# Silu at a block's end moved by a section to ScalarE and GpSimd, and idle transposes at the start, in a fused attention and GEGLU kernel

## The chip, the cores and the metric

The kernel runs on one core of one Trainium2 chip. The core has five engines with their own instruction queues: TensorE (PE; its weight loads are listed as PEld), VectorE (DVE), ScalarE (ACT), GpSimd (POOL) and SyncE (SP), which issues nearly all DMA transfers. Each engine works through its queue in order and waits on semaphores for the others. The metric is the device time of one execution in microseconds (us); lower is better. Each kernel's time is the median of several executions.

## The reference

```python
x = A_x                                    # 1 x 2048 x 576
xn = _layernorm(x, axis=-1)
s = _A_ref(xn, A_wqkv, A_wo)               # attention, 32 heads of 18, output projection
g = _silu(_B_ref(xn, B_w_gate, B_w_up, B_w_down))
return x + s * g
...
def _B_ref(x, w_gate, w_up, w_down):       # hidden size 4608
    return (_gelu(x @ w_gate) * (x @ w_up)) @ w_down
```

`_gelu` is the tanh form. All data is float32.

## The kernel before

The 2048 tokens are worked in four blocks of 512 (`TB`, `NB`). Float32 products are made from pairs of rounded parts, a high and a low one (`hi`/`lo`, `wh`/`wl`, `hh`/`hl`, `dh`/`dl`), each split by two operations, on GpSimd in `split` (L91, L92) or on ScalarE and VectorE in `split_av` (L96, L97).

**First phase** (up to about 199 us). For each block, `load_x` fetches four tiles of 128 tokens, `norm` normalises them on VectorE (the last step is L196), ScalarE copies a strip of 64 columns (L198), and `transposes` turns them on TensorE: 20 transposes of 128x128 (L206) into five PSUM banks `pt`, in the order tile `j`, then bank `k`. So each bank is whole only after the fourth tile. `split_t` takes the banks to SBUF (L160, L161). Then `project` multiplies by the q and k weights (`mm_terms`, L152, bank `po`, three buffers) and `values_of` by the v weights. The identity `ident` of the transposes is made by GpSimd at the very start.

**Main phase.** TensorE's order is written by hand (`manual_schedule`); the other engines' queues are ordered by the scheduler, except where `keep_in_program_order` holds an instruction. The phase is a row of 144 *sections*, 36 for each block of the feed-forward part. A section `n` holds 27 pairs of gate and up matmuls (`gate_up`, L347), interleaved with attention's score matmuls (L632, then exp on ScalarE in L633) and row maximum matmuls (L605, then L606 on VectorE). After the pairs, `activate` computes gelu times up (L360 to L364); then TensorE does attention's value matmuls (L666) and the down matmuls (L377) of an earlier section. `down` is called twice for each pair of sections, for the token halves `js` = (0, 1) and (2, 3); VectorE copies (L381, first step of a block) or adds (L383) the result into the sums tile `Y` (128 x 4 x 576), in pieces of 128x288. `finish` splits the gelu product (`hh`, `hl`) and the down weights (`dh`, `dl`).

At the last step of blocks 0 to 2, `down` also makes the silu, by `gate`: tanh(y/2) on ScalarE (L354), then (tanh + 1) y on VectorE (L355), which is twice the silu; L505 takes the half later. The product goes in place into `Y`, and SyncE stores each 128x576 row block to the DRAM tile `ys` (L392). This happens at the end of two successive sections for each block: sections 36 and 37, 72 and 73, 108 and 109. The last block's sums are gated apart, at the end of the kernel (`finals`).

Later, eight pieces of 128x288 for each block, `load_xy` fetches `x` and `ys` into `xx` and `yy` (pool `op`; one and two buffers), and `project_o` computes the output projection and combines (L505 on VectorE, L506 on GpSimd).

SyncE's queue carries, in order, the key loads `KS`, query loads `q`, value loads `VS`, the raw weights (`raw`, two buffers shared by gate/up and down weights), and the stores.

Of the kernel before, what the change touches and what calls it, by code (L numbers as in the profile page):

```python
# [8 lines left out]
F32 = mybir.dt.float32  # L9
F32R = mybir.dt.float32r  # L10
AF = mybir.ActivationFunctionType
ALU = mybir.AluOpType
# [4 lines left out]
S, D, H, DH, F = 2048, 576, 32, 18, 4608  # L17
P = 128
NT = S // P
TB = 512  # L20
# [31 lines left out]
def f(ap):  # L52
    return ap.bitcast(F32)
# [13 lines left out]
def kernel(ctx: ExitStack, tc: tile.TileContext, x, wqkv, wo, w_gate, w_up, w_down, out):  # L67
    nc = tc.nc
# [13 lines left out]
    ys = dram.tile([S - TB, D], F32, name="ys")  # L82
    xhs = [dram.tile([2, D, TB], F32, name=f"xhs{b}") for b in range(NB)]

    ident = const.tile([P, P], F32, name="ident")
# [13 lines left out]
    def raw_tile(shape, pool=wts):  # L99
        return pool.tile(shape, F32, name="raw", tag="raw", bufs=2)  # L100

    def load_gu(t, keep=lambda i: i):

        raw = raw_tile([P, NC, P])
        for a, w in enumerate((w_gate, w_up)):
            keep(nc.sync.dma_start(raw[HR * a:HR * a + HR], w[:, t * P:(t + 1) * P].rearrange("(k p) n -> p k n", p=HR)))
        return raw, [], []
# [7 lines left out]
    def load_xd(b):  # L115

        xd = [[], []]
        for c in range(0, NC, XG):
            for i in range(2):
                t = wts.tile([P, XG, TB], F32R, name=f"xd{i}_{c}")  # L120
                nc.sync.dma_start(f(t)[0:HR], xhs[b][i, c * HR:(c + XG) * HR, :].rearrange("(k p) t -> p k t", p=HR))
                nc.gpsimd.tensor_copy(t[HR:P], t[0:HR])
                xd[i].append(t)
        return xd
# [6 lines left out]
    with tc.tile_pool(name="pro", bufs=1) as pro, tc.tile_pool(name="pps", bufs=1, space=PSUM) as pps:  # L131
# [25 lines left out]
        def split_t(pt, k, xt):  # L157

            if k < KT:
                nc.scalar.activation(xt[0][:, k, :], pt, AF.Copy)  # L160
                nc.vector.tensor_tensor(xt[1][:, k, :], pt, f(xt[0])[:, k, :], op=ALU.subtract)  # L161
            else:
                tmp = tmp2("t1")
                nc.scalar.activation(xt[2][0:HR, :], pt[0:HR], AF.Copy)
                nc.scalar.activation(tmp[HR:P], pt[HR:P], AF.Copy)
                nc.vector.tensor_tensor(xt[2][HR:P, :], pt[HR:P], f(tmp)[HR:P], op=ALU.subtract)
# [10 lines left out]
        def norm(xr, b, between=None):  # L177
# [20 lines left out]
                nc.scalar.activation(xr[j][:, D:D + HR], xr[j][:, R0:D], AF.Copy)  # L198
            return last

        def transposes(b, xr):
            xt = XT[b % 2]
            pts = [pps.tile([P, TB], F32, name="pt", bufs=KT + 1) for k in range(KT + 1)]
            for j in range(4):
                for k in range(KT + 1):
                    nc.tensor.transpose(pts[k][:, j * P:(j + 1) * P], xr[j][:, k * P:(k + 1) * P], ident)  # L206
            for k in range(KT + 1):
                split_t(pts[k], k, xt)
            return xt
# [74 lines left out]
        t, raw = ahead_qk.pop(0)  # L284
# [10 lines left out]
        for b in range(NB):  # L295
# [23 lines left out]
            if b == 1:  # L319
                XD = load_xd(0)  # L320
            if b == 2:
                ahead = load_gu(0, tc.keep_in_program_order)
# [7 lines left out]
    ffn = ctx.enter_context(tc.tile_pool(name="ffn", bufs=1, reuse_waits="tile"))  # L330
    ps = ctx.enter_context(tc.tile_pool(name="ps", bufs=1, space=PSUM))


    FF = {"w": ahead, "xd": XD, "down": [], "n": 0}
    finals = []

    def gate_up(tag):

        w, xd = FF["w"], FF["xd"]
        pg, pu = (ps.tile([P, TB], F32, name=n, tag=tag, bufs=3 if tag == "m" else 2) for n in ("pg", "pu"))  # L340
        terms = [(wp, *divmod(c, XG), xp) for c in range(NC) for wp, xp in ((0, 0), (1, 0), (0, 1))]

        def pair(i):
            wp, k, c, xp = terms[i]
            for a, o in enumerate((pg, pu)):
                rr = slice(HR * a, HR * a + HR)
                nc.tensor.matmul(o, w[1 + wp][k][rr, c, :], xd[xp][k][rr, c, :], start=(i == 0),  # L347
                                 stop=(i == len(terms) - 1))

        return [lambda i=i: pair(i) for i in range(len(terms))], pg, pu  # L350

    def gate(o, th, yy):

        nc.scalar.activation(th, yy, AF.Tanh, scale=0.5)  # L354
        nc.vector.scalar_tensor_tensor(o, th, 1.0, yy, op0=ALU.add, op1=ALU.mult)  # L355
# [11 lines left out]
    def down(b, r, hs, wd, Y, js):  # L367
        for j in js:
            tt = slice(j * P, (j + 1) * P)
            for c in range(2):  # L370
                cc = slice(288 * c, 288 * c + 288)
                py = ps.tile([P, 288], F32, name="py", tag="s", bufs=2)
                n = 0
                for g in range(G):
                    hh, hl = hs[g]
                    for a, w in ((hh, wd[0]), (hh, wd[1]), (hl, wd[0])):
                        nc.tensor.matmul(py, a[:, tt], w[:, g, cc], start=(n == 0), stop=(n == 3 * G - 1))  # L377
                        n += 1
                yy = Y[:, j, cc]
                if r == 0:  # L380
                    nc.vector.tensor_copy(yy, py)  # L381
                else:
                    nc.vector.tensor_tensor(yy, py, yy, op=ALU.add)  # L383
                if b == NB - 1 and r == NR - 1:
                    finals.append((Y, j, c))
        if b < NB - 1 and r == NR - 1:
            for j in js:
                t = b * 4 + j
                for c in range(2):
                    yy = Y[:, j, 288 * c:288 * c + 288]  # L390
                    gate(yy, ffn.tile([P, 288], F32, name="th"), yy)
                nc.sync.dma_start(ys[t * P:(t + 1) * P, :], Y[:, j, :])  # L392

    def section(specials=(), tag="f", pool=wts):

        n = FF["n"]
        FF["n"] += 1
        b, r = divmod(n // G, NR)
        g = n % G
        pairs, pg, pu = gate_up(tag)  # L400
        if g == 0:
            FF["hs"] = []
            if r == 0:
                FF["Y"] = ffn.tile([P, TB // P, D], F32, name="Y")
        keep = tc.keep_in_program_order if n == NU * NA + len(FIRST) else lambda i: i
        nxt = load_gu((n + 1) % (NR * G), keep) if n + 1 < NF else None
        if nxt:
            for k in range(NG - 1):
                split_gu(nxt, k)
        if g == G - 1:  # L410
            raw = FF["rawd"] = raw_tile([P, G, D], pool)
            nc.sync.dma_start(raw, w_down[r * G * P:(r + 1) * G * P, :].rearrange("(g p) n -> p g n", p=P))
        for p in spread(pairs, specials):
            p()
        if nxt:
            split_gu(nxt, NG - 1)
        FF["w"] = nxt
        if n + 1 < NF and (n + 1) % (NR * G) == 0:
            FF["xd"] = load_xd(b + 1)
        FF["act"] = activate(pg, pu)  # L420
# [20 lines left out]
    op = ctx.enter_context(tc.tile_pool(name="op", bufs=1, reuse_waits="tile"))  # L441
# [79 lines left out]
    def tasks(n, part):  # L521
        for t in todo.pop((n, part), []):
            t()

    S2 = [None]
    for b in range(NB):
# [9 lines left out]
        for i in range(GROUPS):  # L536
            n = first + i
            past = i - (ENDS - 2 - first) if last else -1
            if past >= 0:
                n = ENDS - 2 + past // 2  # L540
# [11 lines left out]
    with tc.tile_pool(name="att", bufs=1, reuse_waits="tile") as att:  # L552
# [32 lines left out]
        def load_q(u):  # L585
            j, g = divmod(u, NQ)
            cols = slice(j * TB, (j + 1) * TB)
            for r in range(2):
                t = QS[u, r] = att.tile([P, TB], F32R, name=f"q{r}", bufs=3)
                for a in range(2):  # L590
                    q = f(t)[64 * a:64 * a + MROW, :]
                    h = QD * g + 2 * r + a
                    rows = slice(h * DH, (h + 1) * DH)
                    for n, i in enumerate((0, 0, 1)):
                        nc.sync.dma_start(q[n * DH:(n + 1) * DH, :], qk[i, rows, cols])
# [118 lines left out]
        for n in range(NU * NA):  # L714
            u, i = divmod(n, NA)
            s0 = n * SLOTS
            section([p for s in range(s0, s0 + SLOTS) for p in slot_pairs(s)])
            if n > 0:
                load_k(n - 1 + KB)
            load_v(n + 2)  # L720
            if i == 1 and u + 2 < NU:
                load_q(u + 2)
            tasks(n, 0)
            um, im = divmod(s0 + LEAD + SLOTS, NS)
            if im == 0 and um <= NU:
                max_neg(um - 1)
            for kt in range(i * SLOTS // 2, (i + 1) * SLOTS // 2):
                values(u, kt)
            if im == 0 and um <= NU:
                max_end(um - 1)  # L730
            tasks(n, 1)
            downs()
            tasks(n, 2)
            finish()


    with tc.tile_pool(name="epi", bufs=1, reuse_waits="tile") as epi:
        S2[0] = epi.tile([P, TB // P, D], F32, name="S2")
        XX = epi.tile([P, TB // P, D], F32, name="XX")
        n = NU * NA  # L740
# [15 lines left out]
        for Y, j, c in finals:  # L756
            cc = slice(288 * c, 288 * c + 288)
            rows = slice(S - TB + j * P, S - TB + (j + 1) * P)
            th = epi.tile([P, 288], F32, name="thl", bufs=len(finals))
# [33 lines left out]
```

## Time and profile before

| | |
|---|---|
| median of 3 runs | 2700.95 us (2699.92 to 2701.48) |
| the profiled execution | 2699.41 us |
| its span in the trace | 2697.6 us |
| mean granted TensorE clock | 0.995 |

A row of a timeline has start (us), duration (us), engine, line, operation, output<-input, shapes and count; in square brackets stands how long the engine was idle before it and which instruction ended that wait. "q" behind an engine's name marks its sequencer, such as the issue of a DMA. A row of a group view has the count, then busy time in us and the mean in ns, then the idle time before it. A row of a tile's view has the smallest, median and largest duration in ns, and the first and last start. L-numbers are lines of the kernel before.

### The profile page before, as it was taken

The numbers are of one execution on the slowest core, as the hardware profiler recorded it, in microseconds if no ns is written. First come the engines' busy times: TensorE is split into PE (matmuls) and PEld (weight loads), VectorE is DVE, ScalarE is ACT, GpSimd is POOL, SyncE is SP. The second block draws the span as 40 slices with busy tenths as digits, with TensorE's granted clock in tenths as the row PEclk, the third lists the DMA queues.
The fourth block names the chain that finished last, engine by engine and source line by source line (L and its number), as shares of the span: only waits on it lengthen the run. The fifth ranks groups of instructions, "written<-read, shape, count | busy, mean of one in ns | idle before, by whom it ended". The sixth has DMA issues, their size and how long they took to land.

```text
span 2697.6 us, 55502 instructions
## 1 busy us (share of the span) xinstructions
PE 2654.8 (98%) x21000; PEld 2041.0 (76%) x21000; DVE 2005.5 (74%) x3430; ACT 1430.2 (53%) x2542; POOL 1363.9 (51%) x1454
## 2 busy tenths in 40 slices
PE   8998999999999999999999999999999999999997
PEld 7887777777777777777777777777777777777676
DVE  6326888888888877788888877888888877888344
ACT  3221355556665555566656554566555555665622
POOL 2116644444465555545456555454456555444563
PEclk9999999999999999999999999999999999999999
DMA  8874433333354334533345344433435445333341
GB/s 256 262 235 125 111 95 102 104 104 103 101 141 116 102 102 119 137 104 103 103 111 147 102 115 128 130 102 99 103 98 138 118 121 140 104 100 87 75 117 39
DMA packets 389144, 323.65 MB, mean 120 GB/s; under 512 B 105544, under 2 KB 302664, under 8 KB 388876
## 3 DMA queue, kind: packets, MB, share of 16 engines
q1 hardware_dynamic: 388876, 320.08, 43.9%
q8 instruction: 167, 2.74, 0.4%
q14 instruction: 101, 0.83, 0.1%
HBM read 266.58 MB, written 52.85 MB: 118 GB/s over the span
## 4 chain that ended last, share of the span: by engine, by line
PE 94%; DVE 3%; POOL 2%; DMA 1%; ACT 1%; issue 0%; SPq 0%; POOLq 0%; DVEq 0%
PE pg L347 27%; PE acc L666 17%; PE py L377 17%; PE pe L632 10%; PE pm L605 9%; PE po L152 7%; PE pu L347 6%; PE po L503 2%; PE pt L206 0%; DMA raw<-in_B_w_up_dram 0%; DVE Y L355 0%; POOL wl L92 0%; DVE mx L606 0%; DVE Y L383 0%; POOL dl L92 0%
## 5 line engine op out<-in xcount | busy, mean ns | idle before, releaser
L633 ACT ACTIVATE pT<-pe 128x512 f32<-128x512 f32 x2048 | 1164.6, 598 | 770.5 <-PE pm L605 551.8
L606 DVE TENSOR_REDUCE mx<-pm 128x1 f32<-128x512 f32 x2048 | 1291.4, 685 | 57.6 <-PE pm L605 35.2
L347 PE MATMUL pg<-xd,wh 64*128 64x512 f32 x2592 | 949.9, 399 | 7.6 <-POOL wh L91 7.6
L347 PE MATMUL pu<-xd,wh 64*128 64x512 f32 x2592 | 950.5, 399 | 0.1
L632 PE MATMUL pe<-q,KS 56*128 56x512 f32 x2048 | 815.3, 406 | 0.1
L605 PE MATMUL pm<-KS,q 54*128 54x512 f32 x2048 | 798.0, 394 | 3.5 <-DVE mx L606 3.0
L91 POOL TENSOR_SCALAR wh<-raw 128x384 fp32r<-128x384 f32 x432 | 221.7, 514 | 888.0 <-DMA raw<-in_B_w_up_dram 505.3
L347 PEld LDWEIGHTS pg<-xd,wh 64*128 64x128 f32 x2592 | 484.5, 187 | 63.5 <-issue 21.1
L347 PE MATMUL pg<-xd,wl 64*128 64x512 f32 x1296 | 510.4, 394 | 1.3 <-POOL wl L92 1.3
L347 PE MATMUL pu<-xd,wl 64*128 64x512 f32 x1296 | 509.0, 393 | 0.0
L347 PEld LDWEIGHTS pu<-xd,wh 64*128 64x128 f32 x2592 | 485.8, 187 | 6.7 <-DVE t L364 1.3
L666 PE MATMUL acc<-pT,VS 128*32 128x512 f32 x4096 | 466.0, 595 | 0.0
L92 POOL TENSOR_TENSOR wl<-raw,wh 128x384 fp32r<-128x384 f32 x432 | 438.1, 1015 | 34.2
L632 PEld LDWEIGHTS pe<-q,KS 56*128 56x128 f32 x2048 | 369.0, 184 | 81.0 <-ACT pT L633 23.0
L383 DVE TENSOR_TENSOR Y<-py,Y 128x288 f32<-128x288 f32 x544 | 248.0, 457 | 207.4 <-PE py L377 206.7
L605 PEld LDWEIGHTS pm<-KS,q 54*128 54x128 f32 x2048 | 376.9, 185 | 33.1 <-DVE mx L606 7.5
L377 PE MATMUL py<-dh,hh 128*128 128x288 f32 x1152 | 358.0, 311 | 4.7 <-ACT dh L96 2.1
L377 PE MATMUL py<-dl,hh 128*128 128x288 f32 x1152 | 340.5, 296 | 3.7 <-POOL dl L92 2.7
L377 PE MATMUL py<-dh,hl 128*128 128x288 f32 x1152 | 339.0, 294 | 0.4 <-POOL hl L92 0.4
L666 PEld LDWEIGHTS acc<-pT,VS 128*32 128x32 f32 x4096 | 120.1, 109 | 276.6 <-issue 265.2
L377 PEld LDWEIGHTS py<-dh,hh 128*128 128x128 f32 x1152 | 216.6, 188 | 82.8 <-issue 44.6
L347 PEld LDWEIGHTS pg<-xd,wl 64*128 64x128 f32 x1296 | 243.1, 188 | 21.4 <-POOL wl L92 2.3
(104 smaller groups left out, 2816.1 us busy)
## 6 DMA issues: line engine op xcount, KB each, us to landing
KS<-qk SPq DMA_DIRECT2D x1536, 36.0 KB
raw<-in_B_w_gate_dram SPq DMA_DIRECT2D x144, 288.0 KB
raw<-in_B_w_up_dram SPq DMA_DIRECT2D x144, 288.0 KB
raw<-in_B_w_down_dram SPq DMA_DIRECT2D x72, 576.0 KB
VS<-vs SPq DMA_DIRECT2D x128, 152.0 KB
qk<-t SPq DMA_DIRECT2D x72, 256.0 KB
q<-qk SPq DMA_DIRECT2D x384, 36.0 KB
xd<-xhs SPq DMA_DIRECT2D x24, 384.0 KB
```

The source lines that it names most:

```text
L91: first = nc.gpsimd.tensor_scalar(hi, raw, 1.0, 1.0, op0=ALU.mult, op1=ALU.mult)
L92: nc.gpsimd.tensor_tensor(lo, raw, f(hi), op=ALU.subtract)
L152: nc.tensor.matmul(o, st, m, start=(i == 0), stop=(i == len(TERMS) - 1))
L347: nc.tensor.matmul(o, w[1 + wp][k][rr, c, :], xd[xp][k][rr, c, :], start=(i == 0), stop=(i == len(terms) - 1))
L377: nc.tensor.matmul(py, a[:, tt], w[:, g, cc], start=(n == 0), stop=(n == 3 * G - 1))
L383: nc.vector.tensor_tensor(yy, py, yy, op=ALU.add)
L503: nc.tensor.matmul(po[:, 0:288], o[x][0:n, k, :], OW[w][0:n, k, :], start=(m == 0), stop=(m == len(terms) - 1))
L605: nc.tensor.matmul(pm, QS[u, r][rr, t * P:(t + 1) * P], KS[(u * NA + c) % KB][r][rr, :], start=True, stop=True)
L606: nc.vector.tensor_reduce(MX[u][:, 2 * r + a, t, c:c + 1], pm, axis=AX.X, op=ALU.max)
L632: nc.tensor.matmul(pe, KS[(u * NA + c) % KB][r][rr, t * P:(t + 1) * P], QS[u, r][rr, :], start=True, stop=True)
L633: nc.scalar.activation(PT[u, kt][:, 2 * r + a, :], pe, AF.Exp, scale=SCALE)
L666: nc.tensor.matmul(ACC[u][32 * a:32 * a + 32, :], VS[(u * NA + c) % VB][:, v:v + 32], pt[:, a, :], start=(kt == 0), stop=(kt == NT - 1), s ...
```

## The change

```diff
+        def warm(n):
+            o = pps.tile([P, TB], F32, name="po", bufs=3)
+            for i in range(n):
+                nc.tensor.transpose(o[:, 0:P], ident, ident)
...
             for j in range(4):
+                if b == 0 and j == 0:
+                    warm(64)
                 for k in range(KT + 1):
...
-    FF = {"w": ahead, "xd": XD, "down": [], "n": 0}
+    FF = {"w": ahead, "xd": XD, "down": [], "gates": [], "n": 0,
+          "Y": ffn.tile([P, TB // P, D], F32, name="Y")}
...
         if b < NB - 1 and r == NR - 1:
-            for j in js:
-                t = b * 4 + j
-                for c in range(2):
-                    yy = Y[:, j, 288 * c:288 * c + 288]
-                    gate(yy, ffn.tile([P, 288], F32, name="th"), yy)
-                nc.sync.dma_start(ys[t * P:(t + 1) * P, :], Y[:, j, :])
+            FF["gates"] += [(b, j, c, Y) for j in js for c in range(2)]
+
+    def gates():
+        for k, (b, j, c, Y) in enumerate(FF["gates"]):
+            rows, cc = slice(b * TB + j * P, b * TB + (j + 1) * P), slice(288 * c, 288 * c + 288)
+            if k < 3:
+                th = op.tile([P, 288], F32, name="th", tag=("yy", "yy", "xx")[k], bufs=(2, 2, 1)[k])
+            else:
+                th = ffn.tile([P, 288], F32, name="th")
+            tc.keep_in_program_order(nc.scalar.activation(th, Y[:, j, cc], AF.Tanh, scale=0.5))
+            nc.gpsimd.tensor_scalar(th, th, 1.0, 1.0, op0=ALU.add, op1=ALU.mult)
+            nc.gpsimd.tensor_tensor(th, th, Y[:, j, cc], op=ALU.mult)
+            nc.sync.dma_start(ys[rows, cc], th)
+        FF["gates"] = []
...
-            if r == 0:
-                FF["Y"] = ffn.tile([P, TB // P, D], F32, name="Y")
...
             if i == 1 and u + 2 < NU:
                 load_q(u + 2)
+            gates()
             tasks(n, 0)
```

`down` now only notes the four pieces of its half; `gates` is called in the following section, after its gate and up matmuls, and works them off: tanh on ScalarE, add one and multiply on GpSimd, and a store of each 128x288 piece. Its result stands in a `th` tile of its own, for which the buffers of `yy` and `xx` and one `th` buffer serve, and `Y` keeps the sums. `Y` is one tile for the whole run instead of one allocated at each block's start. At the first block, 64 transposes of `ident` into a `po` bank, which nobody reads, stand ahead of the first 20 transposes.

In the built program, ScalarE's four tanh stand right behind L362 of the following section, ahead of the next section's exps. GpSimd's eight operations (add, add, product, product, twice) stand behind the splits of two weight groups (`wh`, `wl`) and ahead of `hh`, `hl`, `dh`, `dl`. SyncE's four stores stand two loads ahead of the end of a group of twelve `KS` loads; four `q` loads that stood among the old stores come after them, and the first loads of `xx` and `yy` for a block follow its last stores. VectorE's queue lacks 24 L355 and is the same otherwise.

## The prediction

> **What bounds the kernel now.** I read the page first: busy shares, then the chain that ended last.
>
> ```profile
> span 2697.6 us, 55502 instructions
> PE 2654.8 (98%) x21000; PEld 2041.0 (76%) x21000; DVE 2005.5 (74%) x3430; ACT 1430.2 (53%) x2542; POOL 1363.9 (51%) x1454
> ...
> PE 94%; DVE 3%; POOL 2%; DMA 1%; ACT 1%; issue 0%; SPq 0%; POOLq 0%; DVEq 0%
> ```
>
> TensorE sets the end; work saved on another engine is worth only the TensorE delay that it caused. So I looked for that delay at the two places of the change. A "section" runs one gate_up on TensorE; its length can be read from ScalarE's timeline as the distance of successive L360 rows, since L360 follows the section's last `pg` matmul. Around the end of token block 0 this timeline reads:
>
> ```profile
> 790.47 0.59 ACT L360 ACTIVATE t<-pg 128x512 f32<-128x512 f32 x1
> ...
> 796.50 0.45 ACT L354 ACTIVATE th<-Y 128x288 f32<-128x288 f32 x1 [0.79 <-DVE Y L355]
> 798.16 0.44 ACT L354 ACTIVATE th<-Y 128x288 f32<-128x288 f32 x1 [1.22 <-DVE Y L355]
> ...
> 808.89 0.59 ACT L360 ACTIVATE t<-pg 128x512 f32<-128x512 f32 x1
> 810.24 0.63 ACT L362 ACTIVATE t<-t 128x512 f32<-128x512 f32 x1 [0.75 <-DVE t L361]
> ...
> 827.36 0.59 ACT L360 ACTIVATE t<-pg 128x512 f32<-128x512 f32 x1
> 828.70 0.63 ACT L362 ACTIVATE t<-t 128x512 f32<-128x512 f32 x1 [0.75 <-DVE t L361]
> 834.73 10.09 ACT L633 ACTIVATE pT<-pe 128x512 f32<-128x512 f32 x16 [5.39 <-PE pm L605]
> 844.71 0.59 ACT L360 ACTIVATE t<-pg 128x512 f32<-128x512 f32 x1
> ```
>
> Two sections take 18.42 and 18.47 us, the next one 17.35. What makes them long are the silu steps: VectorE and ScalarE hand them to and fro, each waiting for the other, and the exps (L633) and row maxima (L606) of the new section queue up behind them. VectorE shows the other half:
>
> ```profile
> 796.98 1.15 DVE L355 SCALAR_TENSOR_TENSOR Y<-th,Y 128x288 f32<-128x288 f32 x1
> 798.05 0.45 DVE L383 TENSOR_TENSOR Y<-py,Y 128x288 f32<-128x288 f32 x1
> ...
> 799.23 0.68 DVE L606 TENSOR_REDUCE mx<-pm 128x1 f32<-128x512 f32 x1
> ...
> 831.66 0.46 DVE L381 COPY Y<-py 128x288 f32<-128x288 f32 x1 [0.78 <-PE py L377]
> ...
> 834.76 10.23 DVE L606 TENSOR_REDUCE mx<-pm 128x1 f32<-128x512 f32 x16 [0.24 <-PE pm L605]
> ```
>
> At 834.76 the maxima start right behind TensorE; at 799.23 they start after the last L383 (798.05) and the L355 before it. The ends of blocks 1 and 2, from the same ScalarE view:
>
> ```profile
> 1434.89 0.59 ACT L360 ACTIVATE t<-pg 128x512 f32<-128x512 f32 x1
> ...
> 1452.68 0.59 ACT L360 ACTIVATE t<-pg 128x512 f32<-128x512 f32 x1
> ...
> 1471.18 0.59 ACT L360 ACTIVATE t<-pg 128x512 f32<-128x512 f32 x1
> ```
>
> ```profile
> 2078.50 0.59 ACT L360 ACTIVATE t<-pg 128x512 f32<-128x512 f32 x1
> ...
> 2097.74 0.59 ACT L360 ACTIVATE t<-pg 128x512 f32<-128x512 f32 x1
> ...
> 2116.20 0.59 ACT L360 ACTIVATE t<-pg 128x512 f32<-128x512 f32 x1
> ```
>
> Lengths 17.79, 18.50, 19.24 and 18.46. All six: 110.88; six plain ones would be 6 x 17.35 = 104.10. The silu of three block ends costs TensorE **6.8 us**, 0.25% of the run.
>
> The other place is the start:
>
> ```profile
> 1.01 0.29 POOL masks.py:199 TENSOR_SCALAR_AFFINE_SELECT ident<-ident 128x128 f32<-128x128 f32 x1
> ...
> 10.25 2.05 DVE L196 TENSOR_SCALAR xx<-xx,st 128x576 f32<-128x576 f32 x4
> ...
> 10.97 4.50 PE L206 MATMUL pt<-ident,xx 128*128 128x128 f32 x20 [10.97 <-DVE xx L196]
> ...
> 12.49 0.29 ACT L96 ACTIVATE rest<-raw 128x128 fp32r<-128x128 f32 x1
> 12.81 1.04 DVE L97 TENSOR_TENSOR rest<-raw,rest 128x128 fp32r<-128x128 f32 x1 [0.52 <-ACT rest L96]
> ...
> 14.65 2.07 ACT L160 ACTIVATE xth<-pt 128x512 fp32r<-128x512 f32 x4 [1.87 <-PE pt L206]
> ...
> 17.11 1.09 PE L152 MATMUL po<-xth,ql 128*128 128x512 f32 x4
> ...
> 45.44 2.35 PE L206 MATMUL pt<-ident,xx 128*128 128x128 f32 x20
> ```
>
> The same 20 transposes take 4.50 us at 10.97 and 2.35 at 45.44: 0.225 against 0.118 us each. All inputs are there by 12.3 (10.25 + 2.05), yet ScalarE waits for TensorE until 14.65. TensorE is slow in its first microseconds.
>
> **The change part by part.**
>
> *Removed at block ends.* Per half block, four L355 leave VectorE and four tanh leave the boundary between two sections. VectorE's order is otherwise that of before, so L606 starts as at 834.76 and the six sections come down to 17.35: **-6.8**. A bound from below: were only one of the two hand-offs cured (VectorE's, but not ScalarE's), I would count half, 3.4.
>
> *Moved to ScalarE.* Four tanh of 0.45 (1.8 us) now stand right behind L362 of the section after, from 810.87. In such a stretch ScalarE idles 5.39 us before the next exps (row 834.73), because TensorE is in the value and down matmuls. Cost 0; without that cover 1.8 x 6 = 10.8. Behind the tanh wait exactly those exps.
>
> *Moved to GpSimd.* Each tanh brings an add and a product, 128x288. Nearest rows:
>
> ```profile
> L91 POOL TENSOR_SCALAR wh<-raw 128x384 fp32r<-128x384 f32 x432 | 221.7, 514 | 888.0 <-DMA raw<-in_B_w_up_dram 505.3
> ```
>
> ```profile
> L506 POOL TENSOR_TENSOR yy<-yy,xx x24: 791/804/811, 991.9 to 2277.0; 128x288 f32<-128x288 f32 x24
> ```
>
> ```profile
> 811.35 1.00 POOL L92 TENSOR_TENSOR wl<-raw,wh 128x384 fp32r<-128x384 f32 x1
> 815.13 0.62 POOL L91 TENSOR_SCALAR hh<-t 128x512 fp32r<-128x512 f32 x1 [2.78 <-PE py L377]
> ...
> 818.61 2.75 POOL L92 TENSOR_TENSOR dl<-raw,dh 128x1152 fp32r<-128x1152 f32 x1
> ...
> 829.00 1.01 POOL L92 TENSOR_TENSOR wl<-raw,wh 128x384 fp32r<-128x384 f32 x1
> ...
> 837.62 0.51 POOL L91 TENSOR_SCALAR wh<-raw 128x384 fp32r<-128x384 f32 x1 [4.67 <-PE pu L347]
> ```
>
> The add: 0.514 for 384 columns and 0.62 for 512 give 0.43 for 288 (estimate). The product has its row, 0.80. Four of each: 4.9 us, between `wl` and `hh`, so behind them wait `hh`, `hl`, `dh`, `dl` and the next third group of `wh`, `wl`. First half: the gates run from 812.35 (811.35 + 1.00) to about 817.3; `hh` stood at 815.13 and, with TensorE 1.1 us ahead, could start at 814.1: 2.1 to 3.2 us late. `dl` then ends 823.5 to 824.6 instead of 821.36. Its first reader is a down matmul ahead of the copy L381 at 831.66; value and down matmuls together fill the gap in ScalarE's exps, which began at 829.3 (834.73 - 5.39), so it starts no earlier than that: 4.7 us of slack remain. Second half: gates 830.0 to 834.9, then `hh`, `hl` (about 2 us) to 836.9, still ahead of 837.62, where GpSimd waited for TensorE anyway. Cost 0, at most 6 x 4.9 = 29 were all of it exposed.
>
> *Moved on SyncE.* Two stores of 128x576 per half become four of 128x288 that wait for GpSimd. SyncE is in order; behind them stand two KS loads, a VS load, the rest of `q` and the raw weights.
>
> ```profile
> 818.86 0.34 SPq L392 DMA_DIRECT2D ys<-Y  x1
> ...
> 821.39 0.63 SPq L106 DMA_DIRECT2D raw<-in_B_w_gate_dram  x1
> ```
>
> Before, the queue was held to 818.86 by the same stores; now the last goes out at about 817.3 to 818. The raw weights at 821.39 wait for `dl` (818.61 + 2.75), so they go 2 to 3 us later; they feed splits of the section after next. The first load of `x` for the output projection now follows the stores; its reader L506 stands behind a whole output projection at the end of a later section. The second four tanh, from 829.33 on, wait for the first four stores to land, which left 11 us before. Cost 0.
>
> *The lasting Y tile.* Block b+1 overwrites Y by L381 at 831.66; GpSimd has read that half by 817.3. The old wait for the ys store at the next block's first tile goes too, but held nobody. Cost 0.
>
> *64 idle transposes.* They need only `ident`, ready at 1.30 (1.01 + 0.29). One costs 0.225 at first and 0.118 later. When does the clock rise? The last first-block transposes (up to 15.47) are slow, the matmuls at 17.11 are fast (four in 1.09): 4.5 to 6.1 us after TensorE's start at 10.97. So 20 to 27 of them at 0.225, then 44 to 37 at 0.118 (5.2 to 4.4 us): the idle ones end between 11.0 and 11.8, about when the first real input comes (10.97). The fourth input comes at 12.3; its piece of the first bank is then done by about 12.7, ScalarE is free of L96 at 12.78, and L160 starts near 12.8, not 14.65: -1.85. VectorE's L97 ends at 13.85 and lets the low parts follow 1.44 sooner, against 15.29; they are read last of the three term groups, so I take **-1.8**. Bounds: -1.9, and -0.9 if the idle ones end at 11.8 and sixteen real ones at 0.118 must follow before the first bank is whole (13.7). From 15.47 to the end of the first phase the chain is TensorE alone, so the gain is kept.
>
> The page "TensorE: Matmul & The Clock Gate" of the Trainium skill, section "What's actually happening", says that the clock rises after one busy window of about 3.4 us, and that the windows run freely, so how many matmuls come before the rise varies. By it the time until the rise is 3.4 to 6.8 us instead of 4.5 to 6.1, the idle ones end between 10.5 and 12.1 (an estimate from that page), and this term lies between -0.6 and -1.9. The trace agrees that the rise comes in that reach.
>
> **Sum.** -6.8 - 1.8 = -8.6. The profiled execution took 2699.41 (span 2697.6 and 1.8 around it), the sum gives 2690.8 for it. It lies 1.5 below the median of the runs, 2700.95; for the median I forecast **2692.3**.
>
> **Rivals.**
>
> *Half a cure* (12%): some delay at the section boundary stays, because GpSimd, now busy there, slows VectorE or ScalarE's tanh start late. For it: L355 took 1.15 at 796.98 on a tile for which L383 takes 0.45, so something does slow VectorE there. Against: what VectorE runs there now is L383 and L606, and neither row shows more than its usual time. Time: -3.4 - 1.8, 2695.8.
>
> *No clock for idle work* (5%): were all 64 at 0.225, they would end at 1.30 + 14.4 = 15.7, the real ones 4.7 us late: 2700.95 - 6.8 + 4.7 = 2698.9. Against it: at 10.97 transposes alone, with a few matmuls, raised the clock.
>
> *GpSimd becomes the wait* (7%, the slower one): place, `hh`, `hl`, `dh`, `dl` behind the gates. It decides from the point where the eight operations take 9.6 us (4.9 and the slack of 4.7) rather than 4.9. At 15 us, three times my estimate, the down matmuls of each first half would come 5.4 late, and in the second half `hl` would end at 847 (830.0 + 15 + 2), 2.3 behind L360 at 844.71, which overwrites the tile that `hl` reads: 3 x 7.7 = 23 us, and 2715. For it: these operations on the new tile have no row of their own. Against: the product's row is of the same shape, and half of GpSimd's time is idle.
>
> *The start is absorbed* (6%): -6.8 alone, 2694.1.
>
> The forecast itself has 70%.
>
> **How the numbers follow.** 0.2%, about what a measurement of this kernel can tell from none, is 5.4 us: faster means below 2695.5. The forecast and the absorbed start lie there, and 2 of the 12 points of the half cure, which sits on the border: 0.78. The rest of it and the missing clock are within: 0.15. Slower: 0.07. The range takes the bounds of the start term, the 1.5 us between runs and the half cure, and leaves out the slower rival and the missing clock: 2687.5 to 2697.5.
>
> **What would show it.** In the changed profile: the six L360 distances at 17.3 to 17.6; L606 right behind TensorE after each block end; four tanh in one row after L362; GpSimd's eight operations in 4.9 us, and no TensorE wait for `dl` or `wl` there; idle transposes that end by 11.8, and L160 near 12.8. A distance over 18, or a down matmul waiting for GpSimd, would make the forecast wrong.

## The result, and the profile after

| | before | changed |
|---|---|---|
| median (9 runs each) | 2700.95 us | 2693.05 us |
| lowest to highest | 2699.27 to 2702.02 | 2691.41 to 2695.99 |
| the profiled execution | 2699.41 | 2693.05 |
| its span | 2697.6 | 2691.2 |
| ratio of times | | 0.9972 (95% interval 0.9962 to 0.9982) |

The change saves 7.9 us, 0.28%; 8.6 were forecast, and 2692.3 for the median. Lines have moved: L360, L362 and L364 of before are now L369, L371 and L373, the down copy and add are L390 and L392, exp is L649, row maximum L622, and the new steps are L406 (tanh), L407 (add), L408 (product) and L409 (store). The line of busy times on the page:

```profile
PE 2658.0 (99%) x21064; PEld 2048.6 (76%) x21064; DVE 1995.4 (74%) x3406; ACT 1432.3 (53%) x2542; POOL 1391.6 (52%) x1502
```

TensorE is busy 3 us longer in a span that is 6.4 shorter, but its idle time doesn't show the gain: the 64 idle transposes alone fill 10.0 us in which it had waited. At the block ends it was hardly ever idle, before or after (268.72 busy of 270.09 us before, 263.57 of 263.57 in the changed kernel, in the fifteen sections of the table below): the same number of matmuls took longer with almost no gap between them. So the delay is read from the length of the sections. GpSimd has 48 instructions more, and its busy time grew by 28 us without any visible cost.

ScalarE's timeline of the changed kernel around the end of block 0:

```profile
789.45 0.59 ACT L369 ACTIVATE t<-pg 128x512 f32<-128x512 f32 x1
...
806.80 0.59 ACT L369 ACTIVATE t<-pg 128x512 f32<-128x512 f32 x1
...
808.69 1.43 ACT L406 ACTIVATE th<-Y 128x288 f32<-128x288 f32 x4
814.16 10.08 ACT L649 ACTIVATE pT<-pe 128x512 f32<-128x512 f32 x16 [4.04 <-PE pm L621]
824.14 0.59 ACT L369 ACTIVATE t<-pg 128x512 f32<-128x512 f32 x1
...
841.50 0.59 ACT L369 ACTIVATE t<-pg 128x512 f32<-128x512 f32 x1
```

The four tanh stand in one row behind L371 (808.15) and end at 810.12; ScalarE then still idles 4.04 us before the exps. The sections that were 18.42 and 18.47 are 17.35 and 17.34. The ends of blocks 1 and 2, same view:

```profile
1431.91 0.59 ACT L369 ACTIVATE t<-pg 128x512 f32<-128x512 f32 x1
1449.26 0.59 ACT L369 ACTIVATE t<-pg 128x512 f32<-128x512 f32 x1
...
1466.64 0.59 ACT L369 ACTIVATE t<-pg 128x512 f32<-128x512 f32 x1
```

```profile
2074.43 0.59 ACT L369 ACTIVATE t<-pg 128x512 f32<-128x512 f32 x1
2091.80 0.59 ACT L369 ACTIVATE t<-pg 128x512 f32<-128x512 f32 x1
2109.17 0.59 ACT L369 ACTIVATE t<-pg 128x512 f32<-128x512 f32 x1
```

17.35, 17.38, 17.37, 17.37: the six sections come to 104.16 instead of 110.88. VectorE's timeline shows the boundary as it was meant to be, the maxima directly behind the last add of the sums:

```profile
813.51 0.46 DVE L392 TENSOR_TENSOR Y<-py,Y 128x288 f32<-128x288 f32 x1 [0.34 <-PE py L386]
814.20 10.24 DVE L622 TENSOR_REDUCE mx<-pm 128x1 f32<-128x512 f32 x16 [0.23 <-PE pm L621]
```

GpSimd's timeline, first and second half of block 0, and SyncE's beside the first:

```profile
811.57 0.83 POOL L407 TENSOR_SCALAR th<-th 128x288 f32<-128x288 f32 x2
812.36 1.57 POOL L408 TENSOR_TENSOR th<-th,Y 128x288 f32<-128x288 f32 x2
...
816.25 0.62 POOL L91 TENSOR_SCALAR hh<-t 128x512 fp32r<-128x512 f32 x1
...
819.44 2.68 POOL L92 TENSOR_TENSOR dl<-raw,dh 128x1152 fp32r<-128x1152 f32 x1
...
836.16 1.29 POOL L92 TENSOR_TENSOR hl<-t,hh 128x512 fp32r<-128x512 f32 x1
```

```profile
813.20 3.42 SPq L409 DMA_DIRECT2D ys<-th  x4
...
822.15 0.62 SPq L106 DMA_DIRECT2D raw<-in_B_w_gate_dram  x1
```

The eight operations take 4.7 us (811.57 to 816.25). `dl` ends at 822.12, and the raw weights leave SyncE at once behind it. `hl` of the second half ends at 837.45, 4.05 us ahead of the L369 at 841.50 that overwrites its input.

At the start, all engines' timeline:

```profile
1.36 10.00 PE L205 MATMUL po<-ident 128*128 128x128 f32 x64 [1.36 <-POOL ident masks.py:199]
...
10.48 2.05 DVE L196 TENSOR_SCALAR xx<-xx,st 128x576 f32<-128x576 f32 x4
...
11.20 2.35 PE L214 MATMUL pt<-ident,xx 128*128 128x128 f32 x20
...
13.15 2.07 ACT L160 ACTIVATE xth<-pt 128x512 fp32r<-128x512 f32 x4
```

The idle transposes end at 11.36, the real ones take 2.35 instead of 4.50, L160 starts 1.50 sooner. The inputs (L196) came 0.23 later than in the profile of before.

Three stretches of both profiled executions, the first and second bounded by L360 (L369) rows. "Fifteen sections" are five around each block end, so that a delay that shows a section later is counted too:

| us | before | changed | difference |
|---|---|---|---|
| start of the first L360 (L369) | 206.12 | 205.51 | -0.61 |
| fifteen sections at the three block ends | 270.09 | 263.58 | -6.51 |
| all other time of the span | 2221.4 | 2222.1 | +0.7 |
| span | 2697.6 | 2691.2 | -6.4 |

The profiled execution of before lies 1.5 below its median and that of the changed kernel on it; with this 1.5 the 6.4 are the 7.9 of the medians.

Of the 1.50 won at the start, 0.6 are left at the first L369. The loss stands at the end of the first phase, on VectorE; the same row before, then in the changed kernel:

```profile
184.64 0.69 DVE L253 TENSOR_TENSOR t<-po,t 128x512 fp32r<-128x512 f32 x1 [5.49 <-DMA qk<-t]
```

```profile
184.04 0.69 DVE L261 TENSOR_TENSOR t<-po,t 128x512 fp32r<-128x512 f32 x1 [6.51 <-DMA qk<-t]
```

VectorE waits for the `qk` stores, whose tile it is to fill again, in both kernels; the wait is 1.02 us longer in the changed one, and the row comes 0.60 sooner instead of 1.6 as the row before it did (176.83 against 178.46). TensorE then waits twice, 0.24 and 0.23 us, for a bank that VectorE has not yet emptied. This depends on when transfers land, so the start is judged over several profiles (below).

### The profile page after: what moved, and what is told of

Same layout as the page of the kernel before. It is cut to its first block, busy times and chain, and to the rows that moved or that the text cites. A ratio compares the mean times of both kernels' runs of the same rounds, so it can differ in the third digit from the quotient of the medians.

```text
span 2691.2 us, 55701 instructions
## 1 busy us (share of the span) xinstructions
PE 2658.0 (99%) x21064; PEld 2048.6 (76%) x21064; DVE 1995.4 (74%) x3406; ACT 1432.3 (53%) x2542; POOL 1391.6 (52%) x1502
## 3 DMA queue, kind: packets, MB, share of 16 engines
q1 hardware_dynamic: 390604, 320.08, 44.2%
## 4 chain that ended last, share of the span: by engine, by line
PE 93%; POOL 3%; DMA 2%; DVE 1%; issue 0%; ACT 0%; SPq 0%; POOLq 0%; DVEq 0%; ACTq 0%
PE pg L356 27%; PE acc L682 17%; PE py L386 17%; PE pe L648 10%; PE pm L621 8%; PE po L152 6%; PE pu L356 6%; PE po L519 2%; DMA raw<-in_B_w_up_dram 1%; POOL wl L92 1%; POOL wh L91 0%; PE po L205 0%; DMA qk<-t 0%; PE pt L214 0%; POOL dl L92 0%
## 5 line engine op out<-in xcount | busy, mean ns | idle before, releaser
L649 ACT ACTIVATE pT<-pe 128x512 f32<-128x512 f32 x2048 | 1167.5, 600 | 788.0 <-PE pm L621 601.5
L622 DVE TENSOR_REDUCE mx<-pm 128x1 f32<-128x512 f32 x2048 | 1294.8, 686 | 58.4 <-PE pm L621 35.7
L91 POOL TENSOR_SCALAR wh<-raw 128x384 fp32r<-128x384 f32 x432 | 224.0, 519 | 874.0 <-DMA raw<-in_B_w_up_dram 543.0
L92 POOL TENSOR_TENSOR wl<-raw,wh 128x384 fp32r<-128x384 f32 x432 | 436.9, 1012 | 34.2
L392 DVE TENSOR_TENSOR Y<-py,Y 128x288 f32<-128x288 f32 x544 | 248.4, 458 | 212.8 <-PE py L386 212.2
```

The costliest lines, as they stand in the source:

```text
L91: first = nc.gpsimd.tensor_scalar(hi, raw, 1.0, 1.0, op0=ALU.mult, op1=ALU.mult)
L92: nc.gpsimd.tensor_tensor(lo, raw, f(hi), op=ALU.subtract)
L622: nc.vector.tensor_reduce(MX[u][:, 2 * r + a, t, c:c + 1], pm, axis=AX.X, op=ALU.max)
L649: nc.scalar.activation(PT[u, kt][:, 2 * r + a, :], pe, AF.Exp, scale=SCALE)
```

## The experiments

In the expectations, A is the account held when the run was planned: that of the prediction, except that for the start A has part of the gain taken back at the end of the first phase, where the prediction had it kept. Other letters are rivals, told where they are used. Each set of runs had its own runs of the kernel before on the same chip; differences and ratios are against these, and kernels of different sets are compared by their differences. In all profiles the fifteen sections are measured as above.

**The two parts alone.** Idle transposes in the kernel before:

```diff
+                if b == 0 and j == 0:
+                    warm(64)
```

> The kernel before with the 64 idle transposes alone. Theory A (they raise the clock in time, but part of what they gain is taken back at 180 to 188 us, where TensorE waits for the qk stores): TensorE's first ql matmuls start near 15.6 instead of 17.1 us, the first section near 199.1 instead of 199.7, and the time falls by 0.5 to 1.5 us; the six block-end sections keep their 17.8 to 19.2 us. Rival B (the gain is kept whole): 1.5 to 1.9 us. Rival C (they do nothing): no change.

2698.29 against 2699.57: -1.3, ratio 0.9996 (0.9987 to 1.0005). The fifteen sections stay long, 268.9. The size is as expected, but the interval holds zero. The six sections with the old silu add up to 109.5 us here, where the profile of before has 110.88: the delay differs between executions of the same code, 5.4 us in this one and 6.8 in the other.

The changed kernel without `warm`:

```diff
-                if b == 0 and j == 0:
-                    warm(64)
```

> The changed kernel without the idle transposes. Theory A: the six block-end sections fall to 17.3 to 17.4 us each and the time falls by 6.3 to 7.1 us. Rival: the two parts lean on each other, and the time falls by clearly less than 6 or by the whole 8.

2693.48: -6.1, ratio 0.9979 (0.9970 to 0.9987); fifteen sections 263.3. So the silu's move is the bulk of the change, and by itself.

**Which part of the silu's move?** First without deferral: GpSimd makes the product, but `gates` runs in `down`, where `gate` ran before (no idle transposes).

```diff
         if b < NB - 1 and r == NR - 1:
             FF["gates"] += [(b, j, c, Y) for j in js for c in range(2)]
+            gates()
...
-            gates()
             tasks(n, 0)
```

> As the gates alone, but worked off where the sums end, not a section later: only the engine of the product changes (GpSimd instead of VectorE, a tile of its own instead of the sums tile). Theory A (both hand-offs count: VectorE no longer waits for tanh, but ScalarE's tanh still stand between two sections ahead of the exps, each waiting for its sum): the six sections lie between 17.35 and the old length, about 17.6 to 18.1 each, and the time falls by 3 to 5 us. Rival D (only VectorE's two-way wait matters): the full 6.7. Rival E (only the place matters): no gain.

2694.33: -5.2, ratio 0.9982 (0.9974 to 0.9991); fifteen sections 266.1, between 263.3 and 270.1. ScalarE's timeline from block 0's end on, then a row of VectorE's (L399 is the tanh, L361 what was L360, L642 the exps, L615 the maxima here):

```profile
793.16 0.59 ACT L361 ACTIVATE t<-pg 128x512 f32<-128x512 f32 x1
...
810.53 0.59 ACT L361 ACTIVATE t<-pg 128x512 f32<-128x512 f32 x1
...
817.79 0.45 ACT L399 ACTIVATE th<-Y 128x288 f32<-128x288 f32 x1 [0.36 <-DVE Y L384]
818.14 2.96 ACT L642 ACTIVATE pT<-pe 128x512 f32<-128x512 f32 x5
...
827.90 0.59 ACT L361 ACTIVATE t<-pg 128x512 f32<-128x512 f32 x1
...
845.70 0.59 ACT L361 ACTIVATE t<-pg 128x512 f32<-128x512 f32 x1
```

```profile
817.94 4.53 DVE L615 TENSOR_REDUCE mx<-pm 128x1 f32<-128x512 f32 x7 [0.24 <-PE pm L614]
```

VectorE is on time again (0.24 behind TensorE). Each tanh still waits for one add of the sums and the exps start behind the last of them, but only 0.2 us behind the maxima, and the two sections take 17.37 us each. So do those of the other blocks: the six add up to 104.2, as in the changed kernel. Against the expected 17.6 to 18.1 this is the rival D in these sections: with the product off VectorE, ScalarE's tanh at the boundary cost nothing there. (The product also has a tile of its own now; no run tells the engine from the tile.)

What is left of the delay stands one section later (827.90 to 845.70, 17.80; 17.79 and 19.03 at the other blocks, where the gates alone have 17.4), and it is GpSimd's. At once, the second half's eight operations stand among `hh`, `hl` and `dh`, ahead of `dl`, and TensorE waits for `dl` at all three block ends, 0.2, 0.2 and, at the last, 1.4 us:

```profile
2118.36 0.40 PE L378 MATMUL py<-dl,hh 128*128 128x288 f32 x1 [1.44 <-POOL dl L92]
```

These three sections hold 2.6 of the 2.8 us by which the fifteen are longer than with deferral. So taking the product off VectorE cures the six sections whole, and what the deferral adds, by this profile, is a better time for GpSimd's work. The profiled execution was the slowest of its eleven, 3.8 above their median; by the medians the kernel is 0.9 behind the gates alone, which the intervals don't tell from nothing.

Then the reverse: deferral, but the product stays on VectorE, as one operation in the following section (no idle transposes).

```diff
-            nc.gpsimd.tensor_scalar(th, th, 1.0, 1.0, op0=ALU.add, op1=ALU.mult)
-            nc.gpsimd.tensor_tensor(th, th, Y[:, j, cc], op=ALU.mult)
+            nc.vector.scalar_tensor_tensor(th, th, 1.0, Y[:, j, cc], op0=ALU.add, op1=ALU.mult)
```

> As the gates alone, a section later, but the product stays on VectorE as one instruction instead of two on GpSimd. Theory A (what counts is that tanh and product no longer stand in one another's way at the boundary): VectorE gets 4 x 0.45 us more in a stretch in which it waits for the down matmuls, so the time falls by 5 to 7 us, nearly as with GpSimd. Rival E2 (VectorE has to be freed): 3 or less, since the product stands ahead of the sums and the row maxima of the next section.

2706.63: **+7.1**, ratio 1.0027 (1.0018 to 1.0036); fifteen sections 278.1, 14.8 more than with GpSimd. Rival E2 (VectorE has to be freed) is the nearer one, but it had a gain of 3 or less, not a loss. VectorE's timeline at the end of block 1 (L399 is the product), and a row of GpSimd's beside it:

```profile
1458.50 0.45 DVE L399 SCALAR_TENSOR_TENSOR th<-th,Y 128x288 f32<-128x288 f32 x1
...
1459.46 3.12 DVE L399 SCALAR_TENSOR_TENSOR th<-th,Y 128x288 f32<-128x288 f32 x3
```

```profile
1459.40 1.02 POOL L92 TENSOR_TENSOR wl<-raw,wh 128x384 fp32r<-128x384 f32 x1
```

The first product, started while GpSimd was still idle, takes 0.45; the next three take 1.27, 0.75 and 1.24, a mean of 1.04, beside splits on GpSimd (L91 and L92 at 1459.40 to 1462.26). The Trainium skill, page "SBUF — State Buffer", section "Who interferes with whom", says that a VectorE instruction with two SBUF inputs contends with a GpSimd instruction that reads SBUF, for one port pair that is held for a whole instruction. The rows agree: the two products beside a split L92 (1459.46 and 1461.34) each end 0.3 us behind it. In the changed kernel the add of the sums at 813.51, with one input in PSUM, took its usual 0.46 beside GpSimd's product (812.36 to 813.93). The same shows in the kernel before, whose 24 products had this shape and these inputs (row of the view of L355):

```profile
L355 DVE SCALAR_TENSOR_TENSOR Y<-th,Y x24: 443/722/1155, 795.9 to 2106.9; 128x288 f32<-128x288 f32 x24
```

Those with no GpSimd instruction beside them took 0.45 us, the others up to 1.16. The 1.15 us that the prediction noticed at 796.98 without a cause stands beside two `wl` on GpSimd (796.81, 2.18 for both). So part of the old silu's time was lost in this way; how much of the long sections that makes, no run shows. In the kernel with the product on VectorE, who pays is TensorE:

```profile
1463.00 0.41 PE L378 MATMUL py<-dh,hh 128*128 128x288 f32 x1 [2.06 <-DVE Y L384]
```

```profile
1460.40:1463.81 3.41, 1.35 (x11) 1.12 (x10) 2.91 (x5) 0.00 (x0) 1.78 (x3) 1.00 0.54 168
1463.81:1467.22 3.41, 3.41 (x17) 2.83 (x17) 1.27 (x3) 0.40 (x1) 2.37 (x3) 0.50 0.62 174
```

(The last rows are from the view of stretches: length, then busy time of PE, PEld, DVE, ACT and POOL with their counts, the granted clock, the DMA share and GB/s.) The sums' adds stand behind the products, the down matmuls have two `py` banks, and TensorE stops for 2.06 us. Then the granted clock is 0.50 for 3.4 us, and the down matmuls follow one another every 0.24 us instead of every 0.13. The waits of the whole execution, grouped:

```profile
PE py L378 <- DVE Y L382: 6.1, 4, 2.3
PE py L378 <- DVE Y L384: 4.6, 10, 2.1
```

(us in total, times, longest.) In the changed kernel the same two are 0.3 and 1.6, so the stops are 8.8 of the 14.8; lost clock after three of them is about 5: 3.4 x 0.50 here, and twice some 8 us at a mean granted clock of 0.79, 1.7 each.

**Is GpSimd's slack real, and how large?** Multiplications by one, added to each piece's work on GpSimd:

```diff
             nc.gpsimd.tensor_scalar(th, th, 1.0, 1.0, op0=ALU.add, op1=ALU.mult)
+            for _ in range(6):
+                nc.gpsimd.tensor_scalar(th, th, 1.0, 1.0, op0=ALU.mult, op1=ALU.mult)
```

> The changed kernel with six more 128x288 operations on GpSimd (times one, the result is the same) in each of the four pieces, so that a group of gates takes about 14.5 us instead of 4.7. Theory A (the gates are free because dl has 5.3 us to spare to its first down matmul, 822.1 to 827.4 in the changed kernel's profile, and hl 4.0 us to the next L369 that overwrites its input): the slack is used up, the first halves come 4.5 us late, the second ones 3 to 6, and the time rises by 15 to 30 us over the changed kernel, to 2708 to 2723. Rival (GpSimd has idle time enough in any case): no change, 2693.

2735.98 against 2699.19: +36.8, ratio 1.0134 (1.0119 to 1.0149), where the changed kernel has -7.9: 45 lost, not the 15 to 30 expected; fifteen sections 307.8. Places first. At the end of block 0 this kernel's timelines have, on GpSimd and then on TensorE:

```profile
826.36 2.65 POOL L92 TENSOR_TENSOR dl<-raw,dh 128x1152 fp32r<-128x1152 f32 x1
...
834.52 0.51 POOL L91 TENSOR_SCALAR wh<-raw 128x384 fp32r<-128x384 f32 x1 [3.94 <-PE pm L623]
...
837.66 0.82 POOL L407 TENSOR_SCALAR th<-th 128x288 f32<-128x288 f32 x2
```

```profile
829.06 0.40 PE L386 MATMUL py<-dl,hh 128*128 128x288 f32 x1 [2.73 <-POOL dl L92]
...
858.19 0.61 PE L386 MATMUL py<-dh,hh 128*128 128x288 f32 x1 [9.85 <-DVE Y L390]
```

On SyncE the raw weights, on ScalarE the second half's L369, and for comparison GpSimd's `wh` of the changed kernel:

```profile
829.03 0.64 SPq L106 DMA_DIRECT2D raw<-in_B_w_gate_dram  x1
```

```profile
853.75 0.60 ACT L369 ACTIVATE t<-pg 128x512 f32<-128x512 f32 x1 [10.56 <-POOL hl L92]
```

```profile
827.63 0.51 POOL L91 TENSOR_SCALAR wh<-raw 128x384 fp32r<-128x384 f32 x1 [3.93 <-PE acc L682]
```

`dl`, then `hl` ahead of L369: both as the slower rival named them. But `hl` is 10.56 us late, not 2.3 (and the first half's L369, at 826.46, already waited 3.64 us for its own `hl`). A late `dl` (to 829.01) holds the raw weights (829.03; 822.15 in the changed kernel), these the next `wh` and `wl`: the `wh` starts 5.5 us behind the end of `dl` in both kernels (822.12 to 827.63, 829.01 to 834.52). So the second gates start at 837.66, 11.2 us behind L369, not the 2.6 that I took. And behind the late L369 stand VectorE's copies (L390, 857.70), for which TensorE's two `py` banks wait 9.85 us.

> As the run before with twelve more operations in each piece, 24 us a group. Theory A: beyond the slack each further microsecond of GpSimd costs one, and the weight splits come late too: 50 to 80 us over the changed kernel. Rival: no change.

With twelve multiplications: 2795.28, +96.1, ratio 1.0354 (1.0338 to 1.0369), 104 lost where 50 to 80 were expected; fifteen sections 364.7. Twelve multiplications take 4.79 us (GpSimd's timeline of the kernel with six), so each set of six adds 24 x 6 x 4.79 / 12 = 57.5 us of GpSimd time. The first set costs 307.8 - 263.6 = 44.2 in the sections, the second 56.9. So past the slack GpSimd's time counts one for one, and the hidden part is 57.5 - 44.2 = 13.3 us, 2.2 for each of the six groups. The rows of the changed kernel say the same: from the first group over `dl`, the raw weights and the second group to the second `hl` there is no spare time, and at its end stand 4.05 us, one slack for both groups of a block end. By that 57.5 - 3 x 4.05 = 45.3 would show, and 44.2 do. (TensorE's clock, granted at 0.93 to 0.95 in these sections, is in that sum and not told apart.)

**How many idle transposes?** `warm(128)` and `warm(16)` in the changed kernel.

> The changed kernel with 128 idle transposes instead of 64. Theory A (they end when they end, and the real ones stand behind them): at 0.107 us each the 64 more end near 18.2 us, ScalarE's first L160 starts near 20.2 instead of 13.15, and the time rises by 5 to 7 us over the changed kernel, to 2698 to 2700. Rival: later waits of the first phase hide it, under 2 us.

2696.71: -2.5, ratio 0.9990 (0.9981 to 0.9999), where the changed kernel has -7.9: 5.4 lost, within the 5 to 7 expected (the time itself is under the 2698 to 2700 expected, but so is this set's kernel before, at 2699.19 instead of 2700.95). The start:

```profile
19.15 2.07 ACT L160 ACTIVATE xth<-pt 128x512 fp32r<-128x512 f32 x4 [6.05 <-PE pt L214]
```

L160 is 6.0 later than with 64, and the first L369 starts at 210.51, 5.0 later.

> The changed kernel with 16 idle transposes instead of 64; they end near 4.8 us, and TensorE idles 6 us until the first real input. Theory A (the clock is what they gain, and it falls again in the idle time): the twenty real ones take 4.5 us as in the kernel before, L160 starts near 14.7 to 14.9, and the time is that of the gates alone, 0.5 to 1.5 us over the changed kernel. Rival (something else warms up, such as instruction fetch): L160 near 13.15 as with 64.

2693.12: -6.1, ratio 0.9978 (0.9968 to 0.9987), the gates' part alone.

```profile
1.36 3.39 PE L205 MATMUL po<-ident 128*128 128x128 f32 x16 [1.36 <-POOL ident masks.py:199]
...
11.68 3.79 PE L214 MATMUL pt<-ident,xx 128*128 128x128 f32 x20 [6.93 <-DVE xx L196]
```

After 6.93 us of idle time the real transposes take 3.79, not 2.35. In this profile the clock's column shows why, in a row of the view of stretches:

```profile
7.74:14.57 6.83, 2.89 (x14) 2.90 (x15) 5.14 (x16) 1.96 (x7) 1.34 (x2) 0.50 0.98 215
```

The last two idle transposes are 0.11 us apart instead of 0.21: sixteen were enough to raise the clock, and at 7.74, while TensorE waited, it fell again. So the idle work helps only if it lasts until the first input.

**Is the start's gain kept?** I took the stall at 184 us for `qk` stores behind transfers of the output weights. In two kernels their split, and so the loads, come a block sooner, with 64 idle transposes and with none:

```diff
-                if b == NB - 1 and n < NK:
+                if b == NB - 2 and n < NK:
                     split_wo(n)
```

> The changed kernel with the splitting of the output projection's weights (five loads of wo, ten operations on GpSimd, ten stores to wos) in the third block of the first phase instead of the last. Theory A (the gain of the start is taken back at 182 to 188 us, where qk stores queue behind the wo transfers and VectorE and ScalarE wait for a free tile): no wait of VectorE for a qk store there, the first section starts near 198.1 instead of 199.1 us, and the time falls by 0.5 to 1.5 us against the changed kernel of this set. Rival F (the first sections, bound by loads and GpSimd, take it back in any case): the first section starts earlier, the time is the same.

> As the run before without the idle transposes. Theory A: without the wo transfers in the way, the two runs differ by the whole start term, first section 1.4 to 1.6 us later than there and time 1.0 to 1.8 us longer. Rival F: the first section is later and the time is the same within 0.5 us.

> The changed kernel unchanged, for comparison within one set: 2691.5 to 2694.5, 6.5 to 8.5 us under the kernel before.

> The gates alone once more, in the same set. Theory A (the start term is mostly taken back): 0.3 to 1.3 us over the changed kernel. Rival B (it is kept whole): 1.5 to 1.9 over it.

All four in one set, against 2698.57, with the first L369 of their profiles:

| | time, us | ratio | first L369 |
|---|---|---|---|
| weights sooner, 64 | 2691.11 | 0.9966 (0.9954 to 0.9979) | 204.54 |
| weights sooner, none | 2690.81 | 0.9967 (0.9954 to 0.9979) | 206.94 |
| the changed kernel | 2691.04 | 0.9970 (0.9958 to 0.9982) | 203.36 |
| the changed kernel, none | 2692.96 | 0.9978 (0.9969 to 0.9987) | 207.87 |

In the first, VectorE's wait for the stores has gone from 184 to 137 us with the weights, so it hangs on them, and TensorE waits for none of it. Yet the times with the weights sooner are the same with and without idle transposes, and no better than the changed kernel's. This is what rival F expected (first section sooner, same time), while the pair with the weights as before differs by 1.9, as rival B had it; the intervals are some 3 us wide and don't tell 2 us apart, so the times decide neither. The first L369 does tell the start apart. Over the five profiles with 64 idle transposes and the weights as before (205.51, 204.94, 204.28, 204.96, 203.36) it starts at 204.6 on average; over the five with none (206.12, 206.91, 205.98, 206.43, 207.87) at 206.7. That is **-2.1**, and the two groups don't overlap. The pair with the weights sooner has -2.4.

## Why the prediction was right, step by step

- *Six sections, -6.8.* Measured -6.7 in the changed kernel's profile, with the maxima right behind TensorE. That this is so near is in part luck: both numbers use the one profile of before, and the profile with the idle transposes alone has 5.4 for the same silu. The times of the gates alone, -6.1 and -5.6, lie between. The rival "half a cure" fell. But the step behind its price was wrong: I counted half, 3.4, for VectorE's hand-off cured without ScalarE's. The kernel without deferral is that case, and its six sections are cured whole (104.2). What mattered in them was the product on VectorE; the tanh at the boundary, kept there, cost nothing in them.
- *Tanh on ScalarE, 0.* Right: the four took 1.43 us of the idle time, and 4.04 were left.
- *GpSimd, 0.* The group took 4.7 us where 4.9 were estimated, and nothing was exposed. But the slack is smaller than "4.7 us of slack remain": that row is right for `dl` alone, and I took the two halves as independent. They are coupled through the raw weights; added work was hidden to 2.2 us for each group only. The slower rival named the place and the order and not the price: at 14.1 us for a group (837.66 to 851.79) it costs 45, where 23 was given for 15. The term that failed is the second half's 2.3 us, measured at 10.56.
- *SyncE and the lasting `Y`, 0.* Right: the stores leave by 816.62, the raw weights 0.76 later than before by the clock (2.85 later counted from their section's L369, 806.80 against 808.89), and no TensorE wait for them was added at these places.
- *Idle transposes, -1.8.* They ended at 11.36, within 11.0 to 11.8. L160 came at 13.15, not 12.8: 0.23 of it was the inputs. In this pair of profiles -1.5 at the start and -0.6 at the first section; -2.1 over five against five. "The clock does not rise for idle work" fell: 64 at 0.225 would have ended at 15.7. In time the part shows as -1.3, -1.8 and -1.9 (alone; changed less gates alone; the same in another set) and +0.3 with the weights sooner.

"The gain is kept" to the end of the first phase was right in the mean and wrong in this profile. Whether it is kept to the end is not settled by the times, nor by the rest of the span behind the first L369: that is 2485.7 and 2485.9 in the two profiles of the changed kernel and 2484.8 and 2486.1 in the two without idle transposes, but 2482.6 to 2483.4 in the four with 16 or 128 of them or the weights sooner, whose code from there on is the same. It scatters by more than the 2.1 in question, so this stays open.

The sum, 8.6 against 7.9, came out nearer than its parts: in the profiles the sections gave 6.5, the start 0.6 and the rest lost 0.7, and 1.5 of the 7.9 is where the profiled execution of before lies among its runs.

No kernel that was run is clearly better than the changed one.

## What to carry to other kernels

A hand-off between two engines is read from the length of the bounding engine's sections, not from its busy or idle time: 24 VectorE operations and their tanh cost 5.4 to 6.8 us here with almost no idle time on TensorE, and the same work, deferred but left on VectorE, cost 13 us more than on GpSimd. When the sections named in a theory are cured, look at the next ones too before the rest is put down to the same cause. Before work goes to an engine "half idle", follow what queues behind it and what *those* results release, through the load queue to the next occurrence; slacks in a chain don't stand side by side. Idle matmuls ahead of the first input must end when it comes: 16 helped nothing that shows, 128 cost about 5 us.

## What the runs showed of the hardware

- One VectorE product of 128x288 with both inputs in SBUF took 0.45 us alone and 1.04 on average beside GpSimd's splits.
- A TensorE stop can cost more than its length: after one of 2.06 us the granted clock was 0.50 for 3.4 us, while after the one of 2.73 (to 829.06, above) it stayed at 1.00. The Trainium skill, page "TensorE: Matmul & The Clock Gate", section "What's actually happening", has the clock go down after at least one idle window of about 3.4 us. The 6.93 us ahead of the real transposes with 16 idle ones agree, but the stop of 2.06 is shorter than that page asks, and here the measurement decides.
- The traces show what tells the two stops apart. In each of the fourteen profiles, all changes of the granted clock stand multiples of 3.41 us from one another. Cut into windows at these instants, with the clock at 1.00, it went to 0.50 behind every window in which TensorE was busy for less than 0.45 of the time, and behind none with more than 0.60. The stop of 2.06 us lies whole in one such window (1460.40 to 1463.81 above, busy 1.35 of 3.41); the one of 2.73 us is shared by two, in the kernel with six multiplications:

```profile
823.98:827.40 3.42, 2.34 (x21) 0.58 (x13) 0.31 (x1) 0.60 (x1) 3.42 (x4) 1.00 0.33 118
827.40:830.81 3.41, 1.75 (x13) 1.75 (x14) 2.21 (x4) 1.97 (x5) 3.10 (x3) 1.00 0.06 19
```

- The granted-clock column reads 1.00 ahead of the trace's first record of the clock, whatever the clock is. In the changed kernel's stretches it stands at 1.00 from the start, while the same idle transposes are 0.21 us apart up to about 7.1 us and 0.11 from there on.
